# The first transform of an FFT convolution by even and odd rows: plain float32 on two row halves, an order written by hand, and inputs in contiguous blocks

## The chip, the cores and the metric

The kernel runs on one core of one Trainium2 chip. Time is device time in microseconds (us) of one launch. The kernel before took 1285.75 us, the median of three runs that lay between 1273.37 and 1292.47. The profile shown was taken in an execution of its own, whose time stands in the table below. The engines are called by their names: TensorE (PE in the profile; its weight loads are PEld), VectorE (DVE), ScalarE (ACT), GpSimd (POOL) and SyncE (SP), which here only issues DMAs.

## The reference

The input `x` and `v` have the shape (4, 12800, 128): batch B, sequence S, channels D. The kernel computes a long causal convolution of `u = x * v` with a filter that a small network draws from the positions, gates it by `x`, and passes the result through a short causal convolution with a sigmoid gate and two projections.

```python
h_filt = (np.maximum(pos_emb @ w1, 0.0) @ w2) * np.exp(-0.01 * pos)[:, None]
u = x * v
L = 2 * S
Uf = np.fft.rfft(u, n=L, axis=1)
Hf = np.fft.rfft(h_filt, n=L, axis=0)
y = np.fft.irfft(Uf * Hf[None, :, :], n=L, axis=1)[:, :S, :]
x = x * y                                  # the next part's input
gate_pre = sum(conv_w[k] * xp[:, k:k + S, :] for k in range(5))   # xp: x with 4 zero rows ahead
gate = 1.0 / (1.0 + np.exp(-gate_pre))
out = gate * (x @ w_val) @ w_out
```

`pos_emb` is (12800, 64), `w1` (64, 64), `w2` (64, 128), `w_val` and `w_out` (128, 128), `conv_w` (5, 128). The convolution weights, `w_val` and `w_out` arrive as 64-bit floats and are narrowed on the chip.

## The kernel before, in words

The sequence index is split as j, n1, n2 with J = 2, N1 = 100 and N2 = 64. The Fourier transforms are done in two levels as matrix products, in three phases that follow one another and hand over through DRAM.

**First phase (lines 185 to 308).** The transform over n1. For each k1 of 100, the product with cos and sin of 2 pi n1 (4 k1 + 1) / 400 is needed, so the n1 rows (100 of them) stand on the partitions. The work is cut into 64 *chunks* (j, and two values of n2). Per chunk:
- `fetch` (L244) loads x and v, 100 rows each, into one `ld` tile. Each row is gathered from four batches in pieces of 1 KB. Every such DMA is cut by `_Split` into rows 0 to 95 and 96 to 99, so a chunk has four load instructions on SP's queue.
- `prep` (L252) forms `u_t = x * v` on VectorE (L257), rounds it to the narrower format float32r on ScalarE as `u_hi` (L258), and GpSimd subtracts to get the rest `u_lo` (L259).
- `signal` (L264) forms, for each pair of batches and for cos and sin, three matmuls that add up in one PSUM tile `fp` (L282): high weights by high data, low by high, high by low. ScalarE copies the cos result and VectorE the sin result into `st` (L285, L287). Per chunk four DMAs, two on ScalarE's queue and two on SP's, write `st` to the DRAM tensor `a_u` in pieces of 2 KB.

Beside the signal the filter runs, as a second generator `filt` (L187): 16 position steps (a load of positions; a transpose `tp` on TensorE; a copy `posT` on VectorE; a matmul `gp` with `w1`; rectifier and window on VectorE, L207), then 32 steps of its transform over n1 (`ap`, L221 and L222, whose weights are strided columns of `g_sb`, copied by ScalarE to `ag`), then 25 steps that multiply by the twiddle factors and transform over n2 (`fk` made by ScalarE at L232 and finished by VectorE at L233, then a matmul at L235 and a copy at L237).

The two generators are interleaved by a list of costs and a factor `FS`: the signal makes 128 steps (two per chunk), and after each the filter gets as many of its steps as its share of the summed costs allows. That only sets the program order; in this phase the order in which each engine takes its instructions is then chosen by the compiler's scheduler, which simulates a timeline. Six `ld` buffers are shared by the loads of x and v, positions and later phases.

**Second phase (L314 to L431).** For 50 pairs of k1: `a_u` is loaded (4 KB pieces), transformed over n2 (`z_ps`, on two column halves of TensorE), multiplied with the filter's spectrum by VectorE and GpSimd, transformed back (`c_ps`, L369, on two row halves) and written to `c_y`. Its order is written out by hand.

**Third phase (L441 to L628).** The inverse transform over k1, transposes, the product with x, the short convolution (VectorE, L545), sigmoid, the two projections, the output. Its order is also written out by hand.

## Time and profile before

| | |
|---|---|
| median of three runs | 1285.75 us |
| profiled execution, its own time | 1290.03 us |
| span, first to last instruction | 1288.2 us |
| mean granted TensorE clock | 0.957 of full speed |
| busy, share of the span | PE 91%, DVE 79%, POOL 67%, ACT 49% |
| moved by DMA | 332.95 MB, 258 GB/s over the span |

Rows of groups read: line, engine, operation, tiles out<-in, shapes, count | busy us, mean ns of one | idle time ahead of them and who ended it. A matmul in plain float32 leaves two records, one in float32r leaves one. In stretches, "DMA share" is the mean busy share of the core's 16 DMA engines. Queue q1 is SP's, q10 is ScalarE's. Rows of single instructions begin with the start and the duration in us. Where a line gives three durations with slashes, they are minimum, median and maximum in ns.

### The profile page before, as it was taken

What the parts mean: (1) busy time and instruction counts of PE and PEld (TensorE: products, weight loads), DVE (VectorE), ACT (ScalarE), POOL (GpSimd) and SP (SyncE); (2) the same over time, 40 slices, a digit from 0 to 9 for tenths busy, and PEclk for the clock granted to TensorE, in tenths of its full rate; (3) what the DMA queues carried; (4) which work ended last, traced back from release to release, by engine and by line L of the source; (5) the groups of instructions that cost most, each with busy time, mean ns of one, the idle gap of its engine ahead of it and who ended that gap; (6) DMA issues with size and microseconds to landing.
All of it is one profiled execution on the core that took longest, in us unless ns stands there. A gap on an engine that the chain in (4) does not pass through costs nothing.

```text
span 1288.2 us, 16767 instructions
## 1 busy us (share of the span) xinstructions
PE 1174.3 (91%) x5544; PEld 572.7 (44%) x5544; DVE 1014.1 (79%) x1130; ACT 629.6 (49%) x1064; POOL 867.4 (67%) x346
## 2 busy tenths in 40 slices
PE   4869999978777899999999999989999999999996
PEld 3557776766543233333333333353344444444432
DVE  5856233797655999999999999902999899999897
ACT  3324454677533233333333333304677677667664
POOL 3324233444543689999999999913898898898790
PEclk8979999988978999999999999986999999999999
DMA  9999878889988577788777777645888988999942
GB/s 244 293 298 311 240 238 270 275 259 304 297 260 306 199 263 282 275 286 293 279 278 278 276 276 258 246 142 154 250 270 269 287 255 274 285 272 268 285 142 102
DMA packets 152254, 332.95 MB, mean 258 GB/s; under 512 B 12446, under 2 KB 64714, under 8 KB 150634
## 3 DMA queue, kind: packets, MB, share of 16 engines
q1 hardware_dynamic: 104256, 226.13, 57.8%
q10 hardware_dynamic: 47914, 105.76, 22.7%
q8 instruction: 45, 0.74, 0.2%
q14 instruction: 39, 0.32, 0.1%
HBM read 200.77 MB, written 131.07 MB: 258 GB/s over the span
## 4 chain that ended last, share of the span: by engine, by line
PE 66%; DMA 16%; DVE 8%; issue 3%; POOL 3%; ACT 3%; SPq 1%; ACTq 0%; DVEq 0%; POOLq 0%
PE c_ps L369 14%; PE z_ps L341 13%; PE sd L503 8%; DMA ld<-in_v_dram 7%; PE o_ps L564 7%; PE fp L282 7%; DMA a_u<-st 6%; PE v_ps L554 5%; PE tp L517 4%; PE z_ps L328 3%; DVE gt L545 3%; PE ap L222 2%; PE ap L221 2%; PE o_ps L589 2%; DVE vc L419 1%
## 5 line engine op out<-in xcount | busy, mean ns | idle before, releaser
L530 POOL TENSOR_TENSOR ext<-yr,ld 128x400 f32<-128x400 f32 x120 | 301.6, 2514 | 60.4 <-DVE yr L528 40.5
L259 POOL TENSOR_TENSOR u_lo<-u_t,u_hi 100x1024 fp32r<-100x1024 f32 x64 | 160.0, 2503 | 236.1 <-ACT u_hi L258 212.2
L545 DVE SCALAR_TENSOR_TENSOR gt<-ext,cw,gt 128x1600 f32<-128x1600 f32 x128 | 242.7, 1896 | 0.9 <-ACT gt L542 0.8
L376 ACT COPY c_sb<-c_ps 128x1024 f32<-128x1024 f32 x100 | 101.2, 1012 | 278.4 <-PE c_ps L369 278.4
L341 PE MATMUL z_ps<-ld 128*64 128x512 f32 x800 | 195.3, 607 | 7.7 <-DMA ld<-a_u 6.5
L428 POOL TENSOR_TENSOR va<-va,vb 128x1024 f32<-128x1024 f32 x50 | 156.9, 3138 | 37.0 <-DVE vb L346 36.9
L282 PE MATMUL fp<-u_hi,fwd_hi 100*100 100x512 f32 x256 | 116.9, 456 | 57.5 <-ACT st L285 24.7
L503 PE MATMUL sd<-ld,inv 100*64 100x512 f32 x512 | 146.1, 645 | 2.4 <-DMA ld<-c_y 2.4
L287 DVE COPY st<-fp 100x512 f32<-100x512 f32 x128 | 85.3, 685 | 65.6 <-PE fp L282 57.9
L346 DVE TENSOR_TENSOR vb<-z_ps,h_sb 128x2048 f32<-128x2048 f32 x50 | 114.5, 2291 | 24.6 <-ACT c_sb L376 24.0
L564 PE MATMUL o_ps<-gd,wout 128*128 128x400 f32 x256 | 119.5, 548 | 13.8 <-DVE gd L559 9.4
L429 POOL TENSOR_TENSOR vc<-vc,vd 128x1024 f32<-128x1024 f32 x50 | 118.2, 2365 | 18.6 <-DVE vd L346 13.7
L257 DVE TENSOR_TENSOR u_t<-ld 100x1024 f32<-100x1024 f32 x64 | 86.2, 1348 | 51.7 <-POOL u_lo L259 42.3
L346 DVE TENSOR_TENSOR va<-z_ps,h_sb 128x2048 f32<-128x2048 f32 x50 | 114.1, 2281 | 10.9 <-PE z_ps L341 10.9
L510 ACT COPY sd_sb<-sd 128x512 f32<-128x512 f32 x128 | 75.8, 592 | 88.5 <-PE sd L503 73.6
L430 POOL TENSOR_TENSOR va<-va,vb 128x1024 f32<-128x1024 f32 x50 | 118.4, 2368 | 0.0
L369 PE MATMUL c_ps<-vc,ld 64*128 64x512 f32 x400 | 102.5, 631 | 11.0 <-DVE vc L419 10.6
L282 PE MATMUL fp<-u_hi,fwd_lo 100*100 100x512 f32 x256 | 108.8, 425 | 0.0
L554 PE MATMUL v_ps<-ext,wval 128*128 128x400 f32 x256 | 107.1, 500 | 0.0
L285 ACT COPY st<-fp 100x512 f32<-100x512 f32 x128 | 70.8, 592 | 73.2 <-PE fp L282 44.2
L341 PEld LDWEIGHTS z_ps<-ld 128*64 128x64 f32 x800 | 54.6, 138 | 114.2 <-issue 85.8
L258 ACT CAST u_hi<-u_t 100x1024 fp32r<-100x1024 f32 x64 | 68.2, 1067 | 74.0 <-PE fp L282 31.8
(78 smaller groups left out, 1962.0 us busy)
## 6 DMA issues: line engine op xcount, KB each, us to landing
c_y<-c_sb ACTq DMA_DIRECT2D x100, 512.0 KB
ld<-a_u SPq DMA_DIRECT2D x49, 1024.0 KB
ld<-c_y SPq DMA_DIRECT2D x128, 384.0 KB
ld<-in_xt_dram SPq DMA_DIRECT2D x32, 800.0 KB
out_dram<-o_sb ACTq DMA_DIRECT2D x32, 800.0 KB
ld<-in_x_dram SPq DMA_DIRECT2D x64, 384.0 KB
ld<-in_v_dram SPq DMA_DIRECT2D x64, 384.0 KB
a_u<-st ACTq DMA_DIRECT2D x64, 384.0 KB
```

Of the source, the lines that this page charges most:

```text
L259: nc.gpsimd.tensor_tensor(lo, u_t, hi.bitcast(F32), op=ALU.subtract)
L282: nc.tensor.matmul(out=fp, lhsT=w[:, c], rhs=d[:, b:b + 2], start=(k == 0), stop=(k == 2))
L341: nc.tensor.matmul(out=z[half[h]], lhsT=wk[:, h, half[c]], rhs=a2[:, h, j], start=True, stop=True)
L346: nc.vector.tensor_tensor(out, z.rearrange("p (b d) -> p b d", d=D).unsqueeze(1).to_broadcast([128, n, B, D]), h_sb.unsqueeze(2).to_broadc ...
L369: nc.tensor.matmul(out=c_ps[:, h], lhsT=wk[half[h], 2 + c], rhs=vt[half[h], c].rearrange("p b d -> p (b d)"), start=(c == 0), stop=(c == 1))
L428: nc.gpsimd.tensor_tensor(va[:, 0:2], va[:, 0:2], vb[:, 0:2], op=ALU.add)
L430: nc.gpsimd.tensor_tensor(va[:, 2:4], va[:, 2:4], vb[:, 2:4], op=ALU.add)
L503: nc.tensor.matmul(out=sd[c * N2:(c + 1) * N2], lhsT=inv[:, c], rhs=ct[c][:, r * B * D:(r + 1) * B * D], start=True, stop=True)
L530: nc.gpsimd.tensor_tensor(e[:, r0 + r], yr, xr, op=ALU.mult)
L545: nc.vector.scalar_tensor_tensor(gt, rows(t, k), cw[:, k:k + 1], gt, op0=ALU.mult, op1=ALU.add)
L554: nc.tensor.matmul(out=v_ps, lhsT=wval, rhs=rows(t)[:, r * ROW:(r + 1) * ROW], start=True, stop=True)
L564: nc.tensor.matmul(out=o_ps, lhsT=wout, rhs=gd, start=True, stop=True)
```

## The change

Only the first phase and what feeds it change. The second and third phases have the same text.

- *The transform.* For k1 + 50 the cos and sin factors are those of k1 times (-1)^n1. So the sum over even n1 (`ev`) and the sum over odd n1 (`od`) are formed apart, for k1 below 50 only; their sum gives the rows k1 and their difference the rows k1 + 50. One table `fwd2` holds the cos and sin columns (100 in all) for even n1 on partitions 0 to 49 and for odd n1 on 64 to 113. Per chunk and n2 two matmuls with 50 rows, 100 columns and 512 data columns, in plain float32, stand on two row halves of TensorE. `u_hi`, `u_lo` and the split weights are gone.
- *Around it.* `u_t` is formed per half: the even half by GpSimd always, the odd half by VectorE in odd chunks and by GpSimd in even ones. ScalarE copies `od` out of PSUM (`copy_odd`); VectorE forms `ev + od` and `ev - od` into `st` (`join`); the two halves of `st` are written by ScalarE's and SP's queues.
- *Inputs.* x and v are arranged ahead of the launch into one array, so that each partition row of a chunk is two contiguous pieces of 4 KB; positions come transposed, in 6.4 KB rows, so `tp` and `posT` are gone. A chunk's load is four DMAs: 48 and 2 rows for each parity.
- *Order.* The phase runs under `manual_schedule`: each engine takes its instructions in the order of the program. Loads run four chunks ahead, `prep` two, joins one step behind the matmuls, `fk` one group ahead of its matmul; 14 matmuls on a zero tile stand at the start. `FS` and the cost list have new values, and the narrowing of the three weights is spread over chunks 4, 7 and 10.

```diff
+    half = np.stack([np.cos(th), np.sin(th)], 2)[:, :N1 // 2].reshape(N1 // 2, 2, N1)
+    fwd2 = np.zeros((128, N1))
+    fwd2[:N1 // 2], fwd2[64:64 + N1 // 2] = half[:, 0], half[:, 1]
...
     def dma_start(self, out, in_):
-        for a, b in ((0, 96), (96, N1)):
+        n = out.shape[0]
+        for a, b in ((0, n // 16 * 16), (n // 16 * 16, n)):
             self.eng.dma_start(out=out[a:b], in_=in_[a:b])
...
-                pos_sb = load()[:N1].rearrange("a (j n f) -> a j n f", j=J, f=FO)
-                for j in range(J):
-                    sync_s.dma_start(out=pos_sb[:, j], in_=pos_v[j][:, c0:c0 + HC])
+                pos_sb = load()[:, 0:J * HC // 2 * N1].rearrange("p (j q a) -> p j q a", j=J, q=HC // 2)
+                nc.sync.dma_start(out=pos_sb, in_=post[:, c0 // HC])
...
-                                lhsT=posT[:, q], rhs=w1bd, start=True, stop=True)
+                                lhsT=pos_sb[:, j, n // 2 + q], rhs=w1bd, start=True, stop=True)
...
+            fk = turn(0)
+            yield
+            for k0 in range(0, N1, 4):
+                gz = ps1.tile([128, 4, 2 * N2], F32, name="gp", bufs=2)
+                for i in range(4):
                     nc.tensor.matmul(
-                        out=gz[:, i], lhsT=ag[:, k1].rearrange("p j e -> p (j e)"), rhs=fk[:, i], start=True, stop=True)
+                        out=gz[:, i], lhsT=ag[:, k0 + i].rearrange("p j e -> p (j e)"), rhs=fk[:, i], start=True, stop=True)
+                if k0 + 4 < N1:
+                    fk = turn(k0 + 4)
+                yield
                 nc.scalar.copy(out=ag[:, k0:k0 + 4].rearrange("p k j e -> p k (j e)"), in_=gz)
                 yield
...
+        H1 = N1 // 2
+        par = [slice(h * 64, h * 64 + H1) for h in range(2)]
+
         def fetch(i):
+
             j, n0 = chunks[i]
+            t = load().rearrange("a (w e) -> a w e", w=2)
+            for h in range(2):
+                sync_s.dma_start(out=t[par[h]], in_=xv[j, n0 // P1C, h].rearrange("w a e -> a w e"))
+            return t
 
         def prep(i):
+            t = ahead.pop(0)
+            u_t = p1.tile([128, P1C, B * D], F32, name="u_t", bufs=3)
+            for h, eng in enumerate((nc.gpsimd, nc.vector if i % 2 else nc.gpsimd)):
+                eng.tensor_tensor(
+                    u_t[par[h]].rearrange("a n e -> a (n e)"), t[par[h], 0], t[par[h], 1], op=ALU.mult)
+            return u_t
...
+        def copy_odd(done):
+            od_sb = p1.tile([N1, B * D], F32, name="od_sb", bufs=2)
+            nc.scalar.copy(out=od_sb, in_=done[4])
+            done.append(od_sb)
+
+        def join(done):
+
+            i, n, st, ev, _, od_sb = done
+            nc.vector.tensor_tensor(st[:, 0, n], ev, od_sb, op=ALU.add)
+            nc.vector.tensor_tensor(st[:, 1, n], ev, od_sb, op=ALU.subtract)
+            if n == P1C - 1:
+                j, n0 = chunks[i]
+                for s, eng in enumerate((scalar_s, sync_s)):
+                    eng.dma_start(
+                        out=a_u[s * H1:(s + 1) * H1, :, n0:n0 + P1C, j].rearrange("k c n b d -> (k c) n (b d)"),
+                        in_=st[:, s])
 
         def signal():
+            last = None
+            ready = [prep(0), prep(1)]
+            for i in range(len(chunks)):
+                if i in (4, 7, 10):
+                    weights_in((i - 4) // 3)
+                if i + 4 < len(chunks):
+                    ahead.append(fetch(i + 4))
+                u_t = ready.pop(0)
+                st = p1.tile([N1, 2, P1C, B * D], F32, name="st", bufs=3)
+                for n in range(P1C):
+                    eo = [ps1.tile([N1, B * D], F32, name=nm, bufs=2) for nm in ("ev", "od")]
+                    for h in range(2):
+                        nc.tensor.matmul(out=eo[h], lhsT=fwd2[par[h]], rhs=u_t[par[h], n], start=True, stop=True)
+                    if last:
+                        join(last)
+                    last = [i, n, st, *eo]
+                    copy_odd(last)
+                    if n == 0 and i + 2 < len(chunks):
+                        ready.append(prep(i + 2))
                     yield
+            join(last)
+            yield
+
+        with tc.manual_schedule():
+            ahead = [fetch(i) for i in range(4)]
+            wz = p1.tile([128, 256], F32, name="wz")
+            nc.vector.memset(wz, 0.0)
+
+            for _ in range(14):
+                w_ps = ps1.tile([128, 256], F32, name="gp", bufs=2)
+                nc.tensor.matmul(out=w_ps, lhsT=wz[:, 0:128], rhs=wz, start=True, stop=True)
+
+            FS = 0.97
+            sig, fil = signal(), filt()
+            n_sig = len(chunks) * P1C
+            cost = [0.9, 0.] * (J * N2 // 8) + [0.7, 0.] * (FO // 4) + [1.4, 0.] * (FO // 4) + [0.] + [0.5, 0.5] * (N1 // 4)
...
+    xv = np.stack([np.asarray(inputs[n]).reshape(B, J, N1 // 2, 2, N2 // P1C, P1C, D) for n in ("x", "v")])
+    xv = np.transpose(xv, (2, 5, 4, 0, 3, 6, 1, 7)).reshape(J, N2 // P1C, 2, 2, N1 // 2, -1)
...
+    post = np.transpose(np.asarray(inputs["pos_emb"]).reshape(J, N1, N2 // 16, 8, 2, FO), (4, 5, 2, 0, 3, 1))
```

`turn(k0)` makes the four `fk` of one group by the same ScalarE and VectorE instructions as L232 and L233 before; `weights_in(k)` calls the narrowing of one of the three weights.

109 lines of the change are left out of this document (26 added, 83 removed).

## The prediction

> **What bounds the kernel now.** I read the busy time in stretches first, cut where the first phase changes its side work, then the boundary between the first and the second phase.
>
> ```profile
> span 1288.2 us, 16767 instructions
> core 0: us, PE busy (x) PEld busy (x) DVE busy (x) ACT busy (x) POOL busy (x), PEclk, DMA share, GB/s
> 0.00:130.00 130.00, 93.68 (x530) 69.68 (x531) 88.92 (x138) 46.57 (x69) 45.91 (x23) 0.92 0.97 287
> 130.00:235.00 105.00, 102.62 (x825) 78.12 (x824) 37.53 (x46) 53.81 (x71) 36.13 (x15) 0.98 0.85 252
> 235.00:345.00 110.00, 89.83 (x439) 67.86 (x438) 90.37 (x152) 79.15 (x176) 53.17 (x20) 0.92 0.90 283
> 345.00:404.00 59.00, 42.70 (x146) 26.35 (x144) 28.44 (x33) 22.38 (x34) 24.96 (x11) 0.82 0.83 265
> 399.08 0.73 ACTq L102 DMA_DIRECT2D a_u<-st  x2
> 403.85 2.32 SPq L359 DMA_DIRECT2D ld<-a_u  x5
> ```
>
> The change lies wholly ahead of 403.85, where the second phase's first read of `a_u` is issued; the 884 us behind it stay. Until 130 the DMA is full (share 0.97), from 130 to 235 TensorE is (102.62 of 105, the filter's `ap` matmuls), from 235 to 345, where the filter's `fk` is made, DMA (0.90), VectorE (90.37 of 110) and TensorE are all near full. The chain of waits agrees that loads, stores and `fp` matmuls alternate:
>
> ```profile
> by line: DMA ld<-in_v_dram 23.2%; PE fp L282 20.8%; DMA a_u<-st 17.8%; PE ap L222 6.9%; PE ap L221 5.9%; issue 4.0%; DMA ld<-in_pos_emb_dram 3.1%; DVE u_t L257 2.4%; SPq L102 2.4%; DMA ld<-in_x_dram 2.3%; DVE fk L233 1.7%; ACT st L285 1.4%;
> ```
>
> No one engine can give more than a part; each must be costed anew. A step below is one of the 128 passes of the signal loop, a chunk is two steps.
>
> **TensorE.**
>
> ```profile
> 161.72 0.39 PE L282 MATMUL fp<-u_hi,fwd_hi 100*100 100x512 f32 x1
> 161.95 0.39 PE L282 MATMUL fp<-u_hi,fwd_lo 100*100 100x512 f32 x1
> 526.06 1.99 PE L369 MATMUL c_ps<-vc,ld 64*128 64x512 f32 x8
> 163.02 0.31 PE L222 MATMUL ap<-fwd,g_sb 100*64 100x100 f32 x1
> 163.17 0.31 PE L222 MATMUL ap<-fwd,g_sb 100*64 100x100 f32 x1
> 28.23 1.04 PE L203 MATMUL gp<-w1bd,posT 128*100 128x128 f32 x8
> L235 PE MATMUL gp<-fk,ag 128*128 128x128 f32 x200 | 30.1, 299 | 4.7 <-ACT ag L237 4.7
> L195 PE MATMUL tp<-ident,ld 100*128 100x100 f32 x64 | 8.7, 261 | 1.4 <-DMA ld<-in_pos_emb_dram 1.4
> ```
>
> Before, a step takes six split-float matmuls 0.23 us apart: 1.4 us, 128 x 1.4 = 179. After, it takes one pair in plain float32, 50 rows each, on row halves. The second phase has this form: eight records (two per matmul, so two pairs) in 1.99 us, which is 1.0 a pair, 128 in all. The positions' transposes (8.7) go. What stays: `ap` 384 twin records x 0.147 = 56, `gp` 16 x 1.04 = 17 and `gz` 30. Together 231, under 2 us a step, so the stretch at 130 to 235 no longer ends on TensorE. Each change between tile shapes costs some 0.3 us in estimate (the `ap` record after an `fp` starts 0.1 to 0.2 late), 40 for all; still covered.
>
> **DMA.**
>
> ```profile
> DMA packets 85080, 110.46 MB, mean 273 GB/s; under 512 B 6254, under 2 KB 58522, under 8 KB 84922
> q1 hardware_dynamic: 68944, 82.98, 68.3%
> q10 hardware_dynamic: 16106, 27.11, 21.2%
> DMA packets 30370, 83.58 MB, mean 279 GB/s; under 512 B 1857, under 2 KB 1857, under 8 KB 29326
> q1 hardware_dynamic: 10844, 45.73, 44.4%
> q10 hardware_dynamic: 19506, 37.59, 34.1%
> ```
>
> The first three rows are the first 404 us, the others 500 to 800. Stores cost 0.212 x 404 x 16 / 16106 = 85 ns a packet of about 2 KB, and 84 in the second phase: they stay. Queue q1 in the first phase has 4413 engine-us. Less 12800 store packets at 85 ns and about 160 for the positions, 51200 load packets of 1 KB cost 62 ns each. In the second phase a 4 KB load packet costs 0.444 x 300 x 16 / 10844 = 197 ns. A chunk thus goes from (800 x 62 + 400 x 85) / 16 = 5.2 us to (200 x 197 + 400 x 85) / 16 = 4.6. Over 64 chunks that is 294 against 334. Positions stay at 3.3 MB, some 10 us.
>
> **VectorE, GpSimd and ScalarE.**
>
> ```profile
> L287 DVE COPY st<-fp 100x512 f32<-100x512 f32 x24 | 15.9, 686 | 11.9 <-PE fp L282 10.2 <-DMA a_u<-st 1.7
> L346 DVE TENSOR_TENSOR vc<-z_ps,h_sb x50: 1210/1218/1219, 414.8 to 836.1; 128x1024 f32<-128x1024 f32 x50
> L419 DVE TENSOR_TENSOR vc<-vc,va x50: 1216/1217/3410, 422.1 to 843.2; 128x1024 f32<-128x1024 f32 x50
> L257 DVE TENSOR_TENSOR u_t<-ld x64: 1208/1218/3378, 7.7 to 390.7; 100x1024 f32<-100x1024 f32 x64
> L233 DVE SCALAR_TENSOR_TENSOR fk<-dft,tw,fk x100: 336/342/2480, 16.1 to 331.2; 128x128 f32<-128x128 f32 x100
> L259 POOL TENSOR_TENSOR u_lo<-u_t,u_hi x64: 2351/2394/3637, 13.3 to 394.1; 100x1024 fp32r<-100x1024 f32 x64
> L257 DVE TENSOR_TENSOR u_t<-ld 100x1024 f32<-100x1024 f32 x64 | 86.2, 1348 | 51.7 <-POOL u_lo L259 42.3
> L77 DVE TENSOR_TENSOR top<-top,tmp 128x5 int32<-128x5 int32 x1 | 2.4, 2382 | 0.0
> L233 DVE SCALAR_TENSOR_TENSOR fk<-dft,tw,fk 128x128 f32<-128x128 f32 x92 | 44.9, 538 | 10.1 <-ACT fk L232 10.0
> L285 ACT COPY st<-fp 100x512 f32<-100x512 f32 x128 | 70.8, 592 | 73.2 <-PE fp L282 44.2 <-DMA a_u<-st 8.8 <-DMA ld<-in_pos_emb_dram 6.6
> ```
>
> ScalarE trades two kinds of copy for one, 128 x 0.59 = 76; it is never near full. GpSimd gets 96 products of 1024 elements (three of every four halves) for 64 subtractions, at 2.39 us from `u_lo`: 229. VectorE gets two joins a step, one operand in PSUM. Like the 512-element copy they take 0.68, so 1.36 a step and 174 in all, for 85 of copies; it keeps 32 of the 64 products, which are 1024 elements long whatever the rows, and loses `posT`. The weights' conversions move to chunks 4, 7 and 10; I estimate 14 us for them, three with some ten operations of about 0.2 and one wait like `top`'s 2.4.
>
> The rows of medians and maxima show a trap. With an operand in PSUM (`vc<-z_ps`) VectorE never waits: its longest is 1219. With both in SBUF it goes from 1216 to 3410, from 1208 to 3378, from 336 to 2480: one GpSimd operation more. The Trainium skill, SBUF — State Buffer, "Who interferes with whom", says that such an instruction and a GpSimd one reading SBUF lock each other out for the whole instruction. The trace agrees, and it speaks against the change: the new split products and `fk` run beside a GpSimd that is busier than before. By that rule, pressed to one whole wait for every group, the sum would be the 1313 of the second rival. I take the measured means, 0.538 for `fk` and 1.35 for the product. The bounds are none of the wait (0.34, 1.21) and, on the other side, one whole GpSimd operation for every product and every group of four `fk`.
>
> **The sum by stretches.** The side work is spread by its cost list: 14.4 for positions, 33.6 for `ap`, 25 for `fk`, 73 in all, over 0.97 x 128 = 124 steps. So `fk` begins at step 81.7 and takes 42.5 steps.
> - To step 82, 41 chunks: DMA 41 x 4.6 = 189, four chunks loaded ahead 10, positions 10, tables 2, divided by the best share held (0.97) and 5 for the first load: 222. VectorE there needs 82 x 1.36 + 21 x 1.35 + 16 x 0.69 + 14 = 165, GpSimd 147, TensorE about 170: covered.
> - 42.5 steps with `fk`: VectorE 85 x 0.68 = 58, 10.6 products x 1.35 = 14, 100 x 0.538 = 54, and 8 of waiting for ScalarE's half of `fk` (10.1 before): 134. DMA needs 21 x 4.6 - 10 = 87, so VectorE sets the end.
> - Last 4 steps 9, last store landing 4.
>
> Together 369 for 403.85: 35 less. The profiled execution took 1290.03 (span 1288.2 and 1.8 around it), so 1255. It lay 4.3 above the median of the three, so against 1285.75 I say 1250.
>
> **At nothing.**
>
> ```profile
> 0.74 4.30 DMA ld<-in_x_dram
> 13.26 0.75 PE L282 MATMUL fp<-u_hi,fwd_hi 100*100 100x512 f32 x1 [13.26 <-ACT u_hi L258]
> ```
>
> The first load lands 5 us in, two GpSimd products (4.8) follow, some two microseconds go by between, so the first matmul comes at 12, as before (13.26). The 14 warm-up matmuls of 256 columns lie in that wait; without it they would cost 7 us, 28 records at twice the 0.13 of a `gp` record. The new waits in written order: a store on ScalarE's queue waits for the join's addition, and the next `od` copy stands behind it; a store on SP waits for the subtraction, and the next loads stand behind that. Loads run four chunks (about 20 us) ahead, so SP's wait is hidden; ScalarE's costs VectorE part of the 8 above. At the phase end the first read of `a_u` waits for the last store as now.
>
> **Rivals.**
> - *All waits hide.* `fk` at 0.34, products at 1.21 and no wait for ScalarE: 58 + 13 + 34 = 105, the first stretch 217: 335 in all, 1217 against the median. For it: `fk` before took its waits while `u_lo` depended on `u_t`, a chain that is gone. Against it: the 2480. Chance 0.2.
> - *GpSimd's operations lock VectorE out.* One whole GpSimd operation per group of four `fk`: 25 x 2.39 = 60 beside 34, products at 3.38: 58 + 36 + 94 + 8 = 196, first stretch as above, 431: 1313, the edge of slower. At one and a half, which a GpSimd with two products queued in even chunks would give, 30 more: 1343. It decides from one on. Chance 0.13.
> - *Uneven DMA engines.* GpSimd's row from 235 to 345:
>
> ```profile
> L259 POOL TENSOR_TENSOR u_lo<-u_t,u_hi 100x1024 fp32r<-100x1024 f32 x20 | 53.4, 2672 | 57.1 <-ACT u_hi L258 37.2 <-PE gp L235 15.2 <-DVE fk L233 4.6
> ```
>
>   That is 20 chunks in 110 us, 5.5 each. If the engines that carry the remainder of rows set this, a chunk gave such an engine 28 KB in each of four transfers, 112 KB. The new loads leave 2 rows of 8 KB per half beside 3 on each engine: two engines get 64 KB of loads and 56 of stores, 120 KB, 5.9 us a chunk. 64 x 5.9 + 9 = 387: 1269, no change. For it: with twelve engines carrying 96 KB to the four's 112, the mean share would be (4 + 12 x 96 / 112) / 16 = 0.89, and that stretch has 0.90. Against it: the 0.97 ahead of 130. Chance 0.12. The Trainium skill, DMA: Bandwidth & Descriptors, "Why a DMA increments its semaphore by 16 and not by 1", says that a transfer uses the largest number of engines up to 16 that divides its slowest dimension, the lowest-numbered first; by that rule this rival's uneven load is real, and no view here shows single engines.
> - *Written order loses overlap*, 5.2 us a chunk as before: 25 more, 1275. Chance 0.09. *The row halves don't run together*: 0.9 more a step in the `ap` stretch of 57 steps, 51 more: 1301. The pair at 1.0 us in c_ps speaks against it. Chance 0.04.
>
> **How the numbers follow.** The forecast has 0.42, its own range 1225 to 1275. A difference under 2%, 26 us here, can't be told from none in a measurement of this kernel; that puts the edges at 1260 and 1311. Of the forecast 0.35 lies below 1260; with the first rival, faster has 0.55. Slower has 0.11 from the lock (0.02 of it stays under the edge). The rest, 0.34, is within. The range leaves out a tenth at each end: 1205 (below it only a DMA that also sheds its 0.97) to 1297.
>
> **What would show it.** `a_u` read first near 369 us; pairs of `ev` and `od` near 1.0 us; q1 with about a quarter of the load packets at some 197 ns; joins at 0.68 with no spread; `fk` near 0.54 on average and VectorE fuller than DMA in its steps. A DMA share under 0.9 with no engine full would prove the uneven engines or the written order; `fk` above 0.9, the lock.

## The result and the profile after

The changed kernel takes 1398.55 us, the median of four runs between 1395.39 and 1399.78. The kernel before takes 1287.4 beside it, the median of four between 1273.37 and 1292.47. The ratio is 1.089 with a 95% interval of 1.083 to 1.094: 9% slower, where 3% faster was predicted. (Ratios leave disturbed executions out and medians do not, so a ratio can differ a little from the quotient of two medians.)

The profiled execution of the changed kernel took 1398.79 us, with a span of 1397.0 and a mean granted TensorE clock of 0.861 (0.957 before). Its busy time in stretches, cut at 335 where `fk` begins, and the two issues on SP's queue at the boundary of the phases:

```profile
core 0: us, PE busy (x) PEld busy (x) DVE busy (x) ACT busy (x) POOL busy (x), PEclk, DMA share, GB/s
0.00:25.00 25.00, 10.14 (x32) 6.95 (x32) 3.22 (x6) 1.87 (x2) 10.45 (x9) 0.81 0.89 163
25.00:100.00 75.00, 28.98 (x112) 14.81 (x112) 30.91 (x48) 7.03 (x12) 22.54 (x10) 0.66 0.73 182
100.00:150.00 50.00, 25.83 (x91) 13.38 (x92) 25.12 (x52) 5.27 (x9) 15.37 (x7) 0.67 0.54 141
150.00:335.00 185.00, 175.94 (x1019) 91.06 (x1017) 102.18 (x136) 59.34 (x93) 107.62 (x46) 0.57 0.99 267
335.00:495.00 160.00, 106.50 (x352) 51.39 (x352) 135.70 (x189) 63.55 (x165) 70.08 (x31) 0.67 0.85 206
495.00:513.00 18.00, 10.82 (x40) 4.28 (x40) 10.71 (x17) 4.44 (x8) 1.81 (x1) 0.78 0.64 188
```

```profile
496.97 14.46 SPq L108 DMA_DIRECT2D a_u<-st  x8
512.77 2.32 SPq L377 DMA_DIRECT2D ld<-a_u  x5
```

The second phase's first read of `a_u` is issued at 512.77, before at 403.85. The whole loss of 109 us lies ahead of it: what follows takes 884.2 us of span, before 884.35. The prediction had 369 for this point, made of 222 to the start of `fk`, 134 for the steps with `fk`, and 13 behind them. The trace has 335, 160 and 18, so the errors are 113, 26 and 5.

Three things stand in the stretches. Up to 150 the DMA is not even full (0.73, then 0.54), and no engine is busy either. From 150 to 335 the DMA share is 0.99, yet it moves only 267 GB/s, and TensorE is busy for 175.94 of 185 us at a clock of 0.57. From 335 on VectorE is the fullest engine (135.70 of 160). I take them in this order.

**Up to 150: waits in written order.** The groups by line in this stretch (busy, mean ns of one | idle time ahead and who ended it):

```profile
L191 PE MATMUL gp<-w1bd,ld 128*100 128x128 f32 x119 | 24.6, 373 | 64.4 <-DMA ld<-in_post_dram 64.4
L80 DVE TENSOR_SCALAR top<-raw 128x128 int32<-128x128 int32 x2 | 1.0, 500 | 6.7 <-DMA raw<-in_moe_w_val_dram 3.3 <-DMA raw<-in_moe_w_out_dram 3.3
```

TensorE stands 64.4 us in four waits for the position loads, the longest 24.9. Each of the four is issued by SP where the filter first uses it, behind the loads of x and v that run four chunks ahead. TensorE takes its instructions in program order, so the signal's matmuls stand behind `gp`, and with them the joins and the stores. The narrowing of the weights adds VectorE's waits for `raw`.

**From 150 to 335: dear loads and a slow TensorE.** The queues from 150 to 300 (packets, MB, share of 16 engines), and then the single matmuls of one step among the `ap` matmuls:

```profile
q1 hardware_dynamic: 11049, 29.87, 76.6%
q10 hardware_dynamic: 5280, 9.83, 21.1%
```

```profile
202.57 1.17 PE L293 MATMUL ev<-u_t,fwd 50*100 50x512 f32 x1
202.58 1.17 PE L293 MATMUL od<-u_t,fwd 50*100 50x512 f32 x1
203.54 1.06 PE L293 MATMUL ev<-u_t,fwd 50*100 50x512 f32 x1
203.54 1.06 PE L293 MATMUL od<-u_t,fwd 50*100 50x512 f32 x1
204.53 0.46 PE L210 MATMUL ap<-fwd,g_sb 100*64 100x100 f32 x1
```

Each half of the stores is on one queue, so q10's 9.83 MB are stores alone and q1 has as much of them. Stores thus cost 0.211 x 150 x 16 = 506 engine-us for 4800 pieces of 2 KB, 105 ns a piece. The loads have the rest of q1: (0.766 - 0.211) x 2400 = 1332 engine-us for 20.04 MB, which is 4890 pieces of 4 KB at 272 ns. The prediction had 85 and 197. A chunk costs (200 x 272 + 400 x 105) / 16 = 6.0 us instead of 4.6.

`ev` and `od` start together, so the row halves do run side by side. But a pair takes 204.53 - 202.57 = 1.96 us, twice the 1.0 of the prediction, at a granted clock near one half.

**From 335: `fk`.** Durations of `fk` (minimum/median/maximum) and its group:

```profile
L222 DVE SCALAR_TENSOR_TENSOR fk<-dft,tw,fk x100: 335/350/2532, 335.4 to 494.2; 128x128 f32<-128x128 f32 x100
```

```profile
L222 DVE SCALAR_TENSOR_TENSOR fk<-dft,tw,fk 128x128 f32<-128x128 f32 x100 | 75.1, 806 | 18.1 <-ACT fk L221 18.1
```

The median is 350 ns and the mean 806. If each `fk` either waits for a whole GpSimd operation or not at all, that is (806 - 350) / (2532 - 350), about one in five (an estimate). The waits for ScalarE's half are 18.1 us, where the prediction allowed 8.

What came as predicted: joins at 688 ns, the copy of `od` at 592, GpSimd's products at 2372, the first `ev` matmul at 9.55 us (12 predicted). From the profile's costliest groups:

```profile
L256 POOL TENSOR_TENSOR u_t<-ld 50x1024 f32<-50x1024 f32 x96 | 227.7, 2372 | 268.7 <-PE od L293 118.2
...
L271 DVE TENSOR_TENSOR st<-ev,od_sb 100x512 f32<-100x512 f32 x128 | 88.0, 688 | 104.6 <-ACT od_sb L265 104.0
```

### The profile page after: what moved, and what is told of

The parts are those of the page before. It is cut to its first block, busy times and chain, and to the rows that moved or that the text cites. A ratio compares the mean times of both kernels' runs of the same rounds, so it can differ in the third digit from the quotient of the medians.

```text
span 1397.0 us, 16347 instructions
## 1 busy us (share of the span) xinstructions
PE 1194.8 (86%) x5252; PEld 509.2 (36%) x5252; DVE 1085.0 (78%) x1209; ACT 568.8 (41%) x1000; POOL 930.0 (67%) x378
## 5 line engine op out<-in xcount | busy, mean ns | idle before, releaser
L256 POOL TENSOR_TENSOR u_t<-ld 50x1024 f32<-50x1024 f32 x96 | 227.7, 2372 | 268.7 <-PE od L293 118.2
L548 POOL TENSOR_TENSOR ext<-yr,ld 128x400 f32<-128x400 f32 x120 | 298.6, 2490 | 58.8 <-DVE yr L546 39.0
L293 PE MATMUL ev<-u_t,fwd 50*100 50x512 f32 x256 | 210.3, 933 | 68.0 <-DVE st L272 67.0
L265 ACT COPY od_sb<-od 100x512 f32<-100x512 f32 x128 | 75.5, 592 | 348.9 <-PE od L293 197.9
L293 PE MATMUL od<-u_t,fwd 50*100 50x512 f32 x256 | 210.7, 934 | 1.3 <-POOL u_t L256 1.3
L271 DVE TENSOR_TENSOR st<-ev,od_sb 100x512 f32<-100x512 f32 x128 | 88.0, 688 | 104.6 <-ACT od_sb L265 104.0
L521 PE MATMUL sd<-ld,inv 100*64 100x512 f32 x512 | 142.6, 620 | 4.4 <-DMA ld<-c_y 4.4
L293 PEld LDWEIGHTS ev<-u_t,fwd 50*100 50x100 f32 x256 | 48.8, 234 | 143.7 <-issue 74.8
L387 PE MATMUL c_ps<-va,ld 64*128 64x512 f32 x400 | 99.4, 615 | 0.1
```

Of the source, the lines that this page charges most:

```text
L256: eng.tensor_tensor(u_t[par[h]].rearrange("a n e -> a (n e)"), t[par[h], 0], t[par[h], 1], op=ALU.mult)
L293: nc.tensor.matmul(out=eo[h], lhsT=fwd2[par[h]], rhs=u_t[par[h], n], start=True, stop=True)
L387: nc.tensor.matmul(out=c_ps[:, h], lhsT=wk[half[h], 2 + c], rhs=vt[half[h], c].rearrange("p b d -> p (b d)"), start=(c == 0), stop=(c == 1))
L521: nc.tensor.matmul(out=sd[c * N2:(c + 1) * N2], lhsT=inv[:, c], rhs=ct[c][:, r * B * D:(r + 1) * B * D], start=True, stop=True)
L548: nc.gpsimd.tensor_tensor(e[:, r0 + r], yr, xr, op=ALU.mult)
```

## The experiments

All of them are changes to the changed kernel. The part behind the first read of `a_u` took 875 to 893 us over the runs, so the time of that first read is the cleaner measure; it is called the *boundary* below (512.8 changed, 403.9 before).

### Three single edits: positions, rows of a load, queues

**Positions ahead.** Positions get two buffers of their own, and two of the four loads are issued at the start:

```diff
-                pos_sb = load()[:, 0:J * HC // 2 * N1].rearrange("p (j q a) -> p j q a", j=J, q=HC // 2)
-                nc.sync.dma_start(out=pos_sb, in_=post[:, c0 // HC])
+                pos_sb = pos_t[c0 // HC]
+                if 0 < c0 // HC < 3:
+                    fetch_pos(c0 // HC + 1)
...
+                if i < 2:
+                    fetch_pos(i)
```

> The changed kernel with one edit: the position loads are issued two ahead instead of at the moment of use. Theory A (a load into 48 rows of one partition half runs at about 174 GB/s, as the changed kernel's first 25 us show, and the whole phase is then paced by DMA): the 64.4 us in which TensorE waited for positions shrink to under 10, the first 12 chunks take about 25 + 12 x 6.25 = 100 us in place of 150, and a_u is first read near 460 instead of 513. Theory B (the position waits only used time that the DMA needed anyway): a_u is first read no earlier than 500.

Boundary 482.5, whole 1367.72 (before, on the same chip, 1277.38). TensorE's 64.4 us of waits for positions are gone, but only 30 us of time are. Part of the gap went into the next wait in program order, that of VectorE for the raw weights, here by its group in the first 150 us:

```profile
L80 DVE TENSOR_SCALAR top<-raw 128x128 int32<-128x128 int32 x2 | 0.5, 227 | 21.7 <-DMA raw<-in_moe_w_out_dram 11.5 <-DMA raw<-in_moe_w_val_dram 10.2
```

The result lies between the two expectations. The position waits are one cause and not the only one. (The expectations speak of 174 GB/s in the changed kernel's first 25 us; the stretch above has 163.)

**Loads over all 128 partitions.** x and v are padded ahead of the launch to 64 rows per parity, so that one DMA of 128 rows loads a chunk. That is 28% more bytes:

```diff
-            for h in range(2):
-                sync_s.dma_start(out=t[par[h]], in_=xv[j, n0 // P1C, h].rearrange("w a e -> a w e"))
+            nc.sync.dma_start(out=t, in_=xv[j, n0 // P1C].rearrange("w a e -> a w e"))
...
+    xv = np.pad(xv, ((0, 0),) * 4 + ((0, 14), (0, 0))).reshape(J, N2 // P1C, 2, 128, -1)
```

> The changed kernel with x and v loaded by one DMA of 128 partition rows per chunk (14 unused rows per half, 28% more bytes). Theory A (the half of the partitions limits a load) and theory C (the two remainder rows load two DMA engines unevenly) both expect 256 packets of 4 KB at some 197 ns: (256 x 197 + 400 x 85) / 16 = 5.3 us a chunk in place of 6.25 in the stretch from 150 to 345, loads alone in the first 20 us at 280 GB/s or more in place of 174, a_u first read 30 to 60 us earlier. Theory D (contiguous blocks in DRAM are read slowly): 289 ns a packet as now, 6.8 us a chunk, 35 us or more later.

Boundary 479.3, whole 1365.69: 33 us less in spite of more bytes. The first 25 us, in which little but loads runs, show the rate itself:

```profile
0.00:25.00 25.00, 14.62 (x46) 9.78 (x47) 5.74 (x7) 2.20 (x3) 12.96 (x10) 0.75 0.85 311
```

It is 311 GB/s at a DMA share of 0.85, where the changed kernel had 163 at 0.89. One load of positions (128 rows, 800 KB) is among the 311; from 3 to 8 us, ahead of it, the rates are 412 and 181. The pieces in DRAM are the same 4 KB in both, so it is not the layout in DRAM that makes the loads dear. Whether it is the half of the partitions or the remainder of two rows, this run can't tell.

**Odd rows on ScalarE's queue**, so that loads into both halves are under way at once:

```diff
-                sync_s.dma_start(out=t[par[h]], in_=xv[j, n0 // P1C, h].rearrange("w a e -> a w e"))
+                (sync_s if h == 0 else scalar_s).dma_start(out=t[par[h]], in_=xv[j, n0 // P1C, h].rearrange("w a e -> a w e"))
```

> The changed kernel with the odd half of each load issued on ScalarE's queue, so that both partition halves are written at the same time; rows, remainders and DRAM layout stay. Theory A: 4.6 to 5.2 us a chunk between 150 and 345 (now 6.25), loads alone at 280 GB/s or more, a_u first read 40 to 60 us earlier. Theory C (uneven engines) and theory D (DRAM layout): within 10 us of now, 174 GB/s at the start as now.

Boundary 501.5, whole 1387.61.

```profile
150.00:300.00 150.00, 137.26 (x846) 72.55 (x844) 81.86 (x111) 48.65 (x76) 88.16 (x37) 0.66 0.95 269
```

The rate from 150 to 300 is 269 GB/s, where the changed kernel has 266: a second queue doesn't bring the halves together. (The first 25 us can't be compared, as a load of positions falls into them here and not there.) The 11 us at the boundary go with shorter waits of TensorE for positions, 38.2 us instead of 64.4; their loads stand behind fewer others on SP's queue. The Trainium skill, SBUF — State Buffer, "Can I just issue two DMAs to hit both halves?", says that two transfers to the two halves gave only 6% over one. The trace agrees: 269 against 266 is 1%.

### The three waits and prices together

Positions ahead, 128-row loads, and the raw weights loaded into tiles of their own at the start (the third edit):

```diff
+            for k, w in enumerate((w_val, w_out, conv_w.rearrange("k d -> d k"))):
+                raws.append(p1.tile(list((wval, wout, cw)[k].shape), mybir.dt.int64, name=f"raw{k}"))
+                nc.scalar.dma_start(out=raws[k], in_=w)
```

> The padded load of 128 rows, positions two ahead, and the three 64-bit weights loaded at the start instead of at the moment of their conversion. Theory A with the position waits: start 15, 41 chunks at 5.3 us 217, the stretch with fk about 150 as now, tail 13: a_u first read near 395, the whole kernel near 1280. The granted TensorE clock in the ap stretch rises from 0.5-0.64 to 0.9 or more if the low clock was a consequence of starving; if TensorE itself is what paces (at half clock a step takes 3.3 us), the clock stays near 0.6 and a chunk at 6.2 us or more.

Boundary 449.35, whole 1324.57. The 63 us are the sum of the two single gains, and some 50 us short of what I expected. This kernel, called the *combined* one below, serves as the base for the next four. From 110 to 262, the stretch with `ap`:

```profile
110.00:262.00 152.00, 147.53 (x884) 77.83 (x882) 85.82 (x113) 50.27 (x77) 90.32 (x38) 0.58 0.93 315
```

With the loads cheap, TensorE is the bound: busy 147.53 of 152 at a clock of 0.58. The weights' early loading adds nothing that can be seen at the boundary.

### Four edits of the combined kernel

**ScalarE's half of `fk` in PSUM** (the memory that takes the matmuls' results; the other tiles lie in SBUF). VectorE then reads one operand from PSUM, and one from SBUF:

```diff
+                fp = ps1.tile([128, 4, 2 * N2], F32, name="ap", bufs=2)
...
-                    nc.scalar.activation(fk[:, i], dft[:, 1], AF.Copy, scale=tw[:, 1, k1:k1 + 1])
+                    nc.scalar.activation(fp[:, i], dft[:, 1], AF.Copy, scale=tw[:, 1, k1:k1 + 1])
...
-                        fk[:, i], dft[:, 0], tw[:, 0, k1:k1 + 1], fk[:, i], op0=ALU.mult, op1=ALU.add)
+                        fk[:, i], dft[:, 0], tw[:, 0, k1:k1 + 1], fp[:, i], op0=ALU.mult, op1=ALU.add)
```

> The kernel of the run before (padded load, positions and weights early; a_u first read at 449) with one edit: ScalarE writes its part of fk to PSUM, so VectorE's finishing instruction has one operand in SBUF and one in PSUM. Theory lock (GpSimd's products lock VectorE out of instructions with two SBUF operands): fk falls from 0.81 on average to 0.35 with no maximum near 2.5, VectorE sheds some 45 us between 262 and 449, a_u is first read near 405 to 415. Theory clock (TensorE at half clock paces that stretch too): fk gets as short, but a_u is first read no earlier than 440.

Boundary 439.7, whole 1329.07 (before, beside it, 1288.49; for this run and the next three).

```profile
L222 DVE SCALAR_TENSOR_TENSOR fk<-dft,tw,ap x100: 338/348/349, 272.3 to 419.2; 128x128 f32<-128x128 f32 x100
```

```profile
L222 DVE SCALAR_TENSOR_TENSOR fk<-dft,tw,ap 128x128 f32<-128x128 f32 x100 | 34.7, 347 | 49.3 <-ACT ap L221 49.3
```

The long `fk` are gone: the maximum is 349 ns, and VectorE is busy 41 us less for them. The end moves by 10. The time went into a new wait: VectorE now stands 49.3 us for ScalarE (17.8 in the combined kernel), because the two take turns on one PSUM tile, a quarter of it at a time. The rows of single instructions further down show it.

**Every pair of matmuls issued twice** (the second overwrites the first with the same result):

```diff
-                    for h in range(2):
+                    for h in (0, 1, 0, 1):
```

> The same base (449) with each pair of ev and od matmuls issued twice into the same result. Theory idle (the clock is low because TensorE has too little to do per unit of time, and doubling its work lifts it): granted clock 0.9 or more between 110 and 262, a step there 2 x 1.0 + 1.2 = 3.2 us, as long as now, a_u first read within 20 us of 449. Theory form (pairs on row halves hold the clock down whatever the load): clock 0.5 to 0.6, a step 1.9 us longer, a_u first read 90 us or more later.

```profile
110.00:262.00 152.00, 150.01 (x1104) 86.22 (x1104) 87.78 (x116) 52.45 (x80) 91.95 (x39) 1.00 0.94 314
```

Boundary 473.1, whole 1352.67. With twice the matmuls the clock is 1.00 instead of 0.58, and the boundary comes 24 us later, not 128 x 1.96 = 251 us. So the low clock is not a limit put on a hard-working TensorE; more matmuls per microsecond went with a higher one.

**64 rows per half**, 14 of them zeros from the padding:

```diff
-        par = [slice(h * 64, h * 64 + H1) for h in range(2)]
+        par = [slice(h * 64, h * 64 + 64) for h in range(2)]
```

> The same base (449) with 64 rows per half in the products and in the ev and od matmuls (14 of them zero). Theory rows (the clock counts how much of the array works; 50 of 64 rows is too little, the 64-row pairs of the second phase run at 1.0): clock 0.9 or more between 110 and 262, 2.3 to 2.6 us a step in place of 3.0, a_u first read 20 to 50 us earlier. Theories idle and form: no change, within 8 us, clock 0.6.

```profile
110.00:262.00 152.00, 127.85 (x951) 77.31 (x950) 105.84 (x143) 59.91 (x104) 105.34 (x43) 0.91 0.99 352
```

Boundary 415.67, whole 1298.49: 34 us less for rows of zeros. The clock rises from 0.58 to 0.91, TensorE's share falls, and the DMA is now full at 352 GB/s. The durations of `ev` in this stretch, combined kernel first:

```profile
L291 PE MATMUL ev<-u_t,fwd x101: 589/1057/1173, 110.7 to 261.8; 50*100 50x512 f32 x101
L291 PE MATMUL ev<-u_t,fwd x114: 589/589/1172, 110.2 to 260.4; 64*100 64x512 f32 x114
```

The median falls from 1057 ns to 589. It is 589 as well in the run before, with 50 rows and every pair twice. So a pair is long at the low clock, and not because the row halves fail to run together.

**128 rows cut into two loads of 64**, same bytes, no remainder of rows:

```diff
-            nc.sync.dma_start(out=t, in_=xv[j, n0 // P1C].rearrange("w a e -> a w e"))
+            for h in range(2):
+                hs = slice(h * 64, h * 64 + 64)
+                nc.sync.dma_start(out=t[hs], in_=xv[j, n0 // P1C, :, hs].rearrange("w a e -> a w e"))
```

> The same base (449) with the padded x and v loaded by two DMAs of 64 rows, one per partition half, in place of one of 128. No remainder rows, 4 rows for each DMA engine. Theory A (a load into one half of the partitions is limited to about half the rate): 170 to 230 GB/s in the first 25 us, as in the changed kernel, and 6 us or more a chunk afterwards, a_u first read 20 us or more later. Theory C (only the remainder rows on two engines were slow): 380 GB/s or more as with one DMA, a_u first read within 8 us of 449.

Boundary 470.65, whole 1345.84: 21 us later than the combined kernel. Its first 25 us, and after them those of the combined kernel with one load of 128 rows, each with the same two loads of positions among them:

```profile
0.00:25.00 25.00, 13.70 (x52) 9.87 (x52) 1.93 (x4) 0.00 (x0) 9.39 (x8) 0.85 0.95 221
```

```profile
0.00:25.00 25.00, 13.51 (x52) 9.61 (x52) 1.93 (x4) 1.71 (x2) 15.27 (x10) 0.84 0.94 352
```

The queues from 150 to 300, two loads of 64 first, then one of 128:

```profile
q1 hardware_dynamic: 11923, 34.35, 83.7%
q10 hardware_dynamic: 5154, 9.61, 19.3%
```

```profile
q1 hardware_dynamic: 11796, 34.98, 68.0%
q10 hardware_dynamic: 5104, 9.48, 20.6%
```

Worked as above, a 4 KB piece of a load costs (0.837 - 0.193) x 2400 / 6040 = 256 ns in the first and (0.680 - 0.206) x 2400 / 6226 = 183 in the second. Most of what the changed kernel's 272 has above 183 is thus there without any remainder of rows; by this comparison the remainder is at most the last 16 ns, and the rival of uneven engines falls. One thing isn't told apart: a load of 64 rows fills one half, and it is also a smaller transfer. No run loaded 64 rows that lie in both halves. The Trainium skill, SBUF — State Buffer, "Door 1: The DMA port swizzle (why `[64,N]` ≈ `[32,N]`)", says that partitions 0 to 63 reach only 8 of SBUF's 16 ports and measured 196 GB/s there, against 328 for all 128. The 221 and 352 here agree in kind, with the positions in both.

### The rows alone, and the best of the parts

**64 rows in the changed kernel**, with its loads as they are; three data tiles are zeroed once so that rows 50 to 63 stay zero:

```diff
+            u_ts = [p1.tile([128, P1C, B * D], F32, name=f"u_t{k}") for k in range(3)]
+            for u in u_ts:
+                nc.vector.memset(u, 0.0)
...
-                        nc.tensor.matmul(out=eo[h], lhsT=fwd2[par[h]], rhs=u_t[par[h], n], start=True, stop=True)
+                        nc.tensor.matmul(out=eo[h], lhsT=fwd2[h * 64:h * 64 + 64], rhs=u_t[h * 64:h * 64 + 64, n], start=True, stop=True)
```

> The changed kernel with one edit: 64 rows per half in the ev and od matmuls, the 14 extra rows held at zero; loads, positions and fk as in the changed kernel. Theory rows: the granted clock between 150 and 345 rises from 0.5-0.64 to 0.85 or more. If the slow half loads pace that stretch by themselves (6.25 us a chunk at a DMA share of 0.97 or more), a_u is first read no earlier than 500 (513 now); if the clock paced it, near 475.

Boundary 503.7, whole 1379.7. The stretch from 150 to 300, changed kernel first, then this one:

```profile
150.00:300.00 150.00, 142.89 (x847) 75.00 (x847) 84.87 (x112) 48.66 (x75) 87.43 (x37) 0.59 0.98 266
```

```profile
150.00:300.00 150.00, 119.00 (x886) 69.57 (x884) 81.55 (x116) 48.62 (x79) 91.25 (x38) 0.90 0.98 276
```

The clock goes from 0.59 to 0.90 and TensorE is idle for 31 us instead of 7, but the DMA stays at 0.98 and moves 4% more. Here 9 us come of it, and 34 where loads were cheap. In the changed kernel the two limits were of nearly the same height: with TensorE relieved, the loads hold the stretch up.

**All that helped**: the combined kernel with 64 rows and `fk`'s half in PSUM (both edits as above).

> The base with 64 rows per half (a_u first read at 416) and ScalarE's part of fk in PSUM, together: padded load by one DMA, positions two ahead, weights early, 64 rows, no lock on fk. Theory lock and clock both at work: with the clock at 0.8 or more, taking 46 us of waiting out of fk is no longer hidden by TensorE, as it was where only 10 of them showed (449 to 440). a_u first read near 380, whole kernel near 1262, ratio to the kernel before 0.98. If something else paces the stretch with fk (ScalarE's order, the position of the copies), a_u is first read near 405 and the kernel is the same as before.

Boundary 401.5. The whole is 1285.78, the median of ten, against 1290.16 before; ratio 0.996 [0.991, 1.000], no difference. I had expected 20 us more. The waits from 241 to 390, the stretch with `fk` (us in total, times, longest):

```profile
PE ev L292 <- DVE st L271: 49.2, 27, 4.9
DVE fk L222 <- ACT ap L221: 45.1, 84, 2.0
...
ACT ap L221 <- DVE fk L222: 31.9, 72, 0.9
```

One group of four shows the turns (start and duration, and the wait in brackets):

```profile
303.15 0.35 DVE L222 SCALAR_TENSOR_TENSOR fk<-dft,tw,ap 128x128 f32<-128x128 f32 x1 [0.66 <-ACT ap L221]
303.54 0.37 ACT L221 ACTIVATE ap<-dft,tw 128x128 f32<-128x128 f32 x1 [0.42 <-DVE fk L222]
303.94 0.35 DVE L222 SCALAR_TENSOR_TENSOR fk<-dft,tw,ap 128x128 f32<-128x128 f32 x1 [0.44 <-ACT ap L221]
```

ScalarE does not write the next quarter before VectorE has read the last one, 72 times in the hundred `fk`, and `ev`, the joins and the rest stand behind that in program order. With the tile in SBUF, in the combined kernel, ScalarE wrote four quarters in a row (1.28 us from 356.54), and its hundred writes had 0.0 us of idle time ahead of them.

### The turns taken apart

**ScalarE's part a group ahead.** ScalarE writes all four of a group, and VectorE finishes them half a turn later. Against the run before:

```diff
-                    nc.scalar.activation(fp[:, i], dft[:, 1], AF.Copy, scale=tw[:, 1, k1:k1 + 1])
...
+                    nc.scalar.activation(fp[:, i], dft[:, 1], AF.Copy, scale=tw[:, 1, k0 + i:k0 + i + 1])
+                return fp
+            def finish_turn(k0, fp):
...
-                    fk = turn(k0 + 4)
+                    fp = turn(k0 + 4)
                 yield
                 nc.scalar.copy(out=ag[:, k0:k0 + 4].rearrange("p k j e -> p k (j e)"), in_=gz)
+                if k0 + 4 < N1:
+                    fk = finish_turn(k0 + 4, fp)
```

> The changed kernel with positions loaded two steps ahead, x and v padded to 64 rows per half and loaded as 128 rows, raw weights loaded at the start (the edits of the run with all three), 64-row matmuls, and fk's ScalarE part written to PSUM as in the run before; new is that ScalarE writes its part of a group of four before VectorE finishes the group, so that the two engines no longer take turns on one tile. Theory turns (in the run before the fk stretch was paced by the turns, 46.9 us of VectorE's waits and 33.1 of ScalarE's): a_u first read by the second phase at 380 to 390 (401.5 in the run before), whole 1265 to 1275, fk's wait for ap under 15 us. Rival, loads: a chunk's 1.05 MB take 5.2 us or so at 360 GB/s and this is the bound over most of the phase: a_u no earlier than 398, the whole as before.

Boundary 361.62. The whole is 1237.87, the median of four, against 1284.23 before; ratio 0.970 [0.960, 0.980], faster than both kernels.

```profile
L225 DVE SCALAR_TENSOR_TENSOR fk<-dft,tw,ap 128x128 f32<-128x128 f32 x100 | 28.0, 341 | 8.6 <-ACT ap L219 8.4
```

```profile
200.00:250.00 50.00, 40.39 (x297) 23.83 (x295) 36.60 (x58) 23.95 (x46) 36.15 (x16) 0.97 1.02 382
250.00:300.00 50.00, 36.34 (x163) 18.37 (x164) 42.25 (x89) 30.55 (x74) 33.00 (x14) 0.90 0.99 347
300.00:350.00 50.00, 37.78 (x164) 18.90 (x160) 41.95 (x84) 30.42 (x72) 30.75 (x13) 0.86 0.96 342
```

VectorE's wait for ScalarE falls from 45.1 us to 8.4, and the stretch with `fk` is now full of transfers. The gain at the boundary is 40 us, where I gave the turns 12 to 21. I had left out what stands behind a waiting VectorE in program order: TensorE's waits for the joins (49.2 us above) are 19.6 here, from 236 to 350. The edit does two things, which no run took apart: it ends the turns, and it gives VectorE's part more time behind ScalarE's.

**`fk` spread over more steps**: the cost of each turn in the written order goes from 1.0 to 1.5:

```diff
-            cost = [0.9, 0.] * (J * N2 // 8) + [0.7, 0.] * (FO // 4) + [1.4, 0.] * (FO // 4) + [0.] + [0.5, 0.5] * (N1 // 4)
+            cost = [0.9, 0.] * (J * N2 // 8) + [0.7, 0.] * (FO // 4) + [1.4, 0.] * (FO // 4) + [0.] + [0.75, 0.75] * (N1 // 4)
```

> The run above, with the cost of each turn of fk raised by half in the written order, so that fk is spread over about 54 of the 124 steps instead of 42.5; nothing else differs. Theory turns: with fewer fk per step VectorE's and ScalarE's share of each step falls and the loads of the step hide it: a_u first read at 370 to 385, whole 1255 to 1270. Rival, loads: a step without fk already takes what its loads take, so spreading gains only what fk steps stood above that: a_u 395 to 400 and the whole within 5 us of the run above.

Boundary 360.95. The whole is 1243.7, the median of four; ratio 0.964 [0.953, 0.975], an interval that overlaps the last one. The profile is of an execution of 1254.1.

```profile
250.00:300.00 50.00, 35.87 (x154) 17.25 (x156) 41.62 (x84) 27.89 (x66) 33.68 (x16) 0.90 1.01 362
300.00:350.00 50.00, 36.05 (x152) 16.73 (x148) 40.58 (x80) 26.39 (x62) 35.17 (x15) 0.90 1.01 381
```

`fk` is spread and the DMA is full to the end (1.01), but nothing is won at the boundary. The whole came within 5 us of the run above, as the rival of the loads had it. The boundaries that the two expectations gave (370 to 385, 395 to 400) were both missed, as they were written before the run above was known. Over the first 361 us the DMA share is 0.97 in both runs, at 346 GB/s. That leaves some 11 us of idle DMA, which is about what another order of the same transfers could still win at these prices (an estimate). (A share just over 1 shows how exact this column is.)

## Why the prediction was wrong

The part behind the first phase was right (884 for 884.35), and so were the joins, the copy of `od`, GpSimd's products and the first matmul. The errors, by the prediction's own steps:

- **"To step 82, 41 chunks: DMA", 222 against 335, the step that failed.** The term with the largest error is the price of a chunk, 4.6 us, and in it the load at 197 ns a 4 KB packet. I took that from the second phase's loads of 128 rows and used it for loads that fill one half of the partitions. Those cost 272, and stores beside them 105 instead of 85. The 20.04 MB that came in 150 us are 24.5 chunks of 0.82 MB, 6.1 us a chunk: 41 x 1.5 = 62, and about 4 more for the four chunks loaded ahead (4 x 200 x 272 / 16 = 13.6 for 10). Of these 66 us the loads are 41 x 200 x 75 / 16 = 38 and the 4, and the stores 41 x 400 x 20 / 16 = 21; 3 are left to rounding and idle time. Loads of 128 rows in the same kernel cost 183, so the unit price was right for the shape it was read from. But the runs had them only with 256 packets instead of 200. In the run with ScalarE's part a group ahead they cost 185 from 150 to 300, with stores at 86:

```profile
q1 hardware_dynamic: 14604, 43.28, 80.0%
q10 hardware_dynamic: 6400, 11.90, 20.9%
```

  That is (256 x 185 + 400 x 86) / 16 = 5.1 us a chunk, hardly better than the 5.2 before. The 4.6 existed in neither form, and with it went the whole gain that the prediction gave to the transfers.

  The profile before held a nearer row, which the prediction passed over. In the third phase `c_y` is loaded in 96 and 4 rows and pieces of 4 KB (900 to 1200 us):

```profile
q1 hardware_dynamic: 15678, 61.76, 74.1%
ld<-c_y SPq DMA_DIRECT2D x104, 384.0 KB
ld<-in_xt_dram SPq DMA_DIRECT2D x25, 800.0 KB
```

  The queue took 0.741 x 300 x 16 = 3557 engine-us. The 25 loads of 128 rows are 20.5 MB, 985 engine-us at 197 ns per 4 KB. The rest is 2572 for the 10400 pieces of `c_y`, about 247 ns each (an estimate). Four pieces of 1 KB in the first phase before, also in 96 and 4 rows, cost 4 x 62 = 248. So longer pieces alone were no reason to expect cheaper bytes: at 247 a chunk would have cost (200 x 247 + 400 x 85) / 16 = 5.2 us, as before.
- **"Positions only as 10 us of DMA".** I priced their bytes and not the place of their issue. To 150 us the DMA was busy for 0.89 x 25 + 0.73 x 75 + 0.54 x 50 = 104 us; the other 46 were idle, for the most part behind the four position loads and the weights, and 2 more to 335. The prediction had 11 in all (5 for the first load, and the division by 0.97). The single edit made the boundary 30 us earlier, and the next wait in program order took over. Idle time (48 - 11 = 37) and dear chunks (66) make 103 of the 113; the other 10 are DMA time as well (287 busy to 335, where the sum had 211), and I can't assign them. "Loads run four chunks ahead" was given as what hides SP's waits; it was also what the position loads had to queue behind.
- **TensorE "pair 1.0".** It was 1.96. The term came from the second phase at full clock. Here the clock was 0.57 with 50 of 64 rows, and about 0.9 with all 64. In the changed kernel this decided little (9 us when mended alone), because the loads were as slow. With cheap loads it was the bound, and worth 34.
- **"42.5 steps with fk: 134", 160 in fact.** `fk` took 806 ns on average and not 538. By the mean alone that is 27 us, which equals the error of this stretch (26) only by luck, since other terms were off as well. In the busy times `fk` is 75.1 us instead of 54 (some durations overlap), the waits for ScalarE are 18.1 and 6.7 instead of 8, and the joins and products take 135.7 - 75.1 = 60.6 instead of 72: 21 + 17 - 11 is 27. So the lock, which the second rival described, was real: 100 x (0.806 - 0.342) / 25 = 1.86 us for each group of four, 0.78 of a GpSimd operation of 2.39. It stayed under the point "above 0.9" that the prediction had set. The argument that `fk` "took its waits while `u_lo` depended on `u_t`, a chain that is gone" pointed the wrong way. Without the lock most of the same time went into waiting for ScalarE (49.3 us instead of 17.8).
- **The rivals.** "All waits hide" fell. "Uneven DMA engines" fell with the 128 rows cut in two, which have no remainder and cost nearly as much a piece (256 against 272 ns). "The row halves don't run together" fell with the matmuls at 202.57 and 202.58 and with the 589 ns of the run with 64 rows. "Written order loses overlap" had the right mechanism, at 25 us where the idle time alone was 37 above the sum. No rival had the price of a half-filled load, the largest part of the error. It is not the only one: 66 us less would be 1333, still above the 1297 where the range ends.

That the last kernels reach the boundary at 361, near the 369 of the prediction, doesn't bear out its sum: their chunks cost 5.1 us and not 4.6, and positions, clock and `fk` had to be mended first.

What stays open: what sets the price of a `st` piece (85 ns before, 105 in the changed kernel; with loads of 128 rows 107 in the combined kernel and 86 with ScalarE's part a group ahead), how much of 272 against 256 is the remainder of rows, and what counts in a load, the half or the smaller transfer. The 247 for 96 and 4 rows, which reach into both halves, suggest that it is not the half alone.

## What to carry to other kernels

Take a transfer's price only from a row with the same partitions: a 4 KB piece of a load into one half of SBUF cost 256 to 272 ns here, and 183 in a load over all 128. When an order is written by hand, list for every queue what an instruction stands behind at its place of issue, the small loads above all: here the late ones stopped all engines, one after the other. Mend the limits together before judging one, since an edit that gave 9 us alone gave 34 once the limit beside it was gone, and taking two engines' turns apart gave 40 where removing the lock with GpSimd had given 10.

## What the runs showed of the hardware that I had not expected

- **Fewer than all partitions.** A 4 KB piece took 272 ns of engine time in loads of 48 and 2 rows into each half, 256 in loads of 64 rows, and 183 in loads of 128. With the DMA share at 0.98 and 0.99, the changed kernel moved 266 GB/s and the run with 64 rows and full loads 352. Two queues don't change it (269). "Busy" DMA engines are thus no sign of bytes moved.
- **The granted clock rose with rows and with matmuls.** 50 rows per half gave 0.58 with TensorE busy for 147.53 of 152 us. 64 rows, 14 of them zeros, gave 0.91, and twice the matmuls 1.00. The Trainium skill, TensorE: Matmul & The Clock Gate, "Part 1: The HAM clock gate (the "warmup" mystery)", says that the clock is gated to half by default and released by how busy TensorE has been. The trace agrees that work releases it, but the profile's busy share isn't that measure: TensorE was busy for 147.53, 127.85 and 150.01 of the 152 us at clocks of 0.58, 0.91 and 1.00. Which quantity it is wasn't found; rows in use and matmuls per time both move it.
- **Turns on one PSUM tile.** Two engines that write and read quarters of one tile alternately waited 45.1 and 31.9 us for each other over a hundred operations of 0.35 us. With ScalarE's four of a group written ahead, VectorE waited 8.4. The profile infers such waits from semaphores; whether the chip needs them or only the program asks for them, no run shows.
